# Two gated spectral filters on one core: a third fold for the even columns, row sums spread by broadcast stationary operands, the l = 512 products on GpSimd, and the inverse two pairs later

## The chip, the core and the metric

The kernel runs on one core of one Trainium2 chip. The core has five engines, each with an instruction queue of its own: TensorE (PE in the profile; PEld is its weight load), VectorE (DVE), ScalarE (ACT), GpSimd (POOL) and SyncE (SP), which here only starts transfers. They work on SBUF, 128 partitions wide; TensorE writes to PSUM, eight banks of 512 f32 columns, from which VectorE and ScalarE copy. Sixteen DMA engines move data. The metric is device time per execution in microseconds: the median of 3 runs before the change is 128.11 (127.71 to 128.34).

## The reference

One input x (2048 x 1024, bf16) goes through two filters, A and B, and a gate per row mixes them:

```python
X = rfft2(x)                      # over rows and columns, in f32
y = irfft2(X * (w_r + 1j * w_i))  # for A and for B, 2048 x 513 weights each
g = sigmoid((x * gate_w).sum(-1)) # one number per row
out = g * a + (1 - g) * b
```

Both filters share the forward transform, so there is one forward and one inverse chain; the gate enters the inverse as a factor on its coefficients.

## The kernel before

Work is written down operation by operation in program order; each names its engine, and waits are derived from which operations wrote or read the same piece. Each engine takes its operations strictly in that order, so the order of the calls sets what queues behind what. Nothing is planned by a scheduler.

**Load and stage 1.** x comes in eight pieces on SP's queue, then the weights in six groups (`wload`: columns t = 0; 1 to 3; 4 to 7; 8 to 11; 12, 13; 14, 15), 8.4 MB that are on their way until 48.7 us. VectorE folds each row twice (`fold`, L334): the row and its mirror image, as sum and difference. `stage1` multiplies with M (L369) and leaves the result in FT, in four blocks (`cmb`, for even and odd columns of the cosine and sine part) of two halves j. ScalarE copies most of PSUM to FT (L378), VectorE the rest (L376).

**Forward pairs.** 16 pairs i = (half hf, p), two t each. `step(i)` does `stage4(i)` (L442, eviction L446 to XF, the tile X), `swap(i)`, two DMAs that exchange the partitions of real and imaginary part (into MM, the tile XS; on GpSimd's queue for i < 8, on SP's from then on), and `stage2(i + 2)` (L418, eviction L427). Stage 2 sums over 256 folded columns for every l, in two matmuls j = 0, 1 of 128 columns each. X and XS have six slots. `product(i, sw)` on VectorE (L459) multiplies X (sw = 0) or XS (sw = 1) with the weights of both filters. Products of hf = 1 use column 512 of the weight rows, which the star products need first: so `star_products` (L493) waits for all weights, saves what it needs, and copies column 256 over column 512 (L496).

**Gate.** `gate_spectrum` (L471) sums the gate's products beside steps 0 to 5; `row_sums` makes 2048 row sums from these on VectorE (AT); `row_spread(hf)` (L502) lays half of them out on a diagonal mask, `zsum` (L508) sums this over partitions with a matrix of ones, ScalarE takes the sigmoid (L511), `gate_mask` (L517) splits it, and `rbgen(r)` (L548) multiplies it into the coefficients of row block r, from U5 (2 MB, loaded after the last stage 2 into FT).

**Inverse.** `group(u, g)` is 16 matmuls of 128 columns (L561) and one eviction (L571, on VectorE L569): 16 groups for hf = 0, which need all products of hf = 0, then 16 for hf = 1. `col0` (L535) corrects column 0 with the star products (PST); it stands before group 0, the last of hf = 0. From `STEP5 = 12` on, groups and steps alternate on TensorE. Then `stage6(r)` (L682, eviction L692) and `stage7(r)` (L707) for 16 row blocks. A row block of the usual kind makes four parts, which VectorE (L754) and then GpSimd (L759) add and subtract; one in `HALF` has VectorE do all of that, at more TensorE time; 14 and 15 are done on VectorE too. SP stores each block.

## Time and profile before

| | |
|---|---|
| median of 3 runs | 128.11 us |
| the profiled execution | 127.73 us, span 125.6 us |
| granted TensorE clock | 1.00 |
| TensorE / VectorE / ScalarE / GpSimd busy | 114.5 / 100.7 / 96.8 / 37.9 us |
| loads on the chain: x, weights | until 9.8 us, until 48.7 us |
| products on VectorE, 32 | 1.23 us each, L459 |
| first inverse group of hf = 1 | 73.03 us |
| first stage 6 | 89.88 us |
| GpSimd's 20 operations of stage 7 | 1.28 us each, 94.9 to 120.8 us |

Times inside the execution count from the span's start. The profiled execution is one of the program, with its span on the core and a little around it that the span does not hold (2.1 us). The chain of waits is followed back from the last instruction; a line of it names what the end was waiting for. A line number L... is that of the kernel before, shown above.

### The profile page before, as it was taken

To read this page: it belongs to the slowest core of one execution; us is meant where nothing else is said; L and a number is where in the kernel's file an instruction comes from. 1 tells how busy PE (TensorE), PEld (TensorE's weight loads), DVE (VectorE), ACT (ScalarE), POOL (GpSimd) and SP (SyncE) were. 2 spreads that over 40 slices of the span, in tenths; PEclk is the share of its full clock that TensorE was granted. 3 is DMA by queue.
4 is the path that set the end of the run, shared out by engine and by line. 5 is a ranking of instruction groups with operands and counts; after the bars stand their busy time and mean duration, and the time that the engine had idled before them with its cause. 6 is when DMAs were issued, how large, how long until landed. Compare 5 with 4: busy or idle time off the path is not lost.

```text
span 125.6 us, 3569 instructions
## 1 busy us (share of the span) xinstructions
PE 114.5 (91%) x1510; PEld 97.6 (78%) x1510; DVE 100.7 (80%) x145; ACT 96.8 (77%) x116; POOL 37.9 (30%) x45
## 2 busy tenths in 40 slices
PE   0399999999999999989999989999799999999980
PEld 0268787887767866979889989999799988998640
DVE  0578999355398988999999999999845788868892
ACT  4229985668989999989899998788669878686630
POOL 1000062006463900000000000000007999979940
PEclk9999999999999999999999999999999999999999
DMA  3999999999999998412894900000000224442366
GB/s 86 327 382 430 416 345 359 347 350 348 360 364 358 358 371 329 160 50 94 297 398 137 317 20 0 5 0 0 5 0 5 84 99 167 157 167 84 113 238 239
DMA packets 17503, 26.27 MB, mean 209 GB/s; under 512 B 2000, under 2 KB 10960, under 8 KB 17360
## 3 DMA queue, kind: packets, MB, share of 16 engines
q1 hardware_dynamic: 16512, 23.81, 54.2%
q0 software_dynamic: 832, 2.11, 4.7%
q8 instruction: 12, 0.20, 0.6%
q10 hardware_dynamic: 144, 0.13, 0.5%
q14 instruction: 3, 0.02, 0.1%
HBM read 17.64 MB, written 4.19 MB: 174 GB/s over the span
## 4 chain that ended last, share of the span: by engine, by line
PE 43%; DVE 28%; DMA 11%; SPq 10%; issue 3%; ACT 2%; DVEq 0%
PE PS L707 13%; PE PS L561 13%; PE PS L682 12%; SPq L280 10%; DVE WB L459 9%; DVE WA L459 8%; DMA WB<-in_A_x_dram 5%; DMA WA<-in_B_w_i_dram 5%; DVE XF L334 5%; DVE FT L376 2%; PE PS L369 2%; PE PS L442 1%; PE PS L418 1%; DVE WA L718 1%; DVE VD L502 1%
## 5 line engine op out<-in xcount | busy, mean ns | idle before, releaser
L759 POOL TENSOR_TENSOR WA<-WA 128x512 bf16<-128x512 f32 x20 | 24.9, 1276 | 51.8 <-DVE WA L754 51.7
L561 PE MATMUL PS<-CL,WB 128*128 128x128 bf16 x256 | 32.4, 226 | 0.5 <-ACT WB L571 0.5
L561 PEld LDWEIGHTS PS<-CL,WB 128*128 128x128 bf16 x256 | 31.5, 145 | 1.4 <-ACT WB L571 0.8
L561 PE MATMUL PS<-CL,WA 128*128 128x128 bf16 x256 | 32.3, 223 | 0.3 <-DVE WA L459 0.3
L561 PEld LDWEIGHTS PS<-CL,WA 128*128 128x128 bf16 x256 | 31.4, 145 | 0.8 <-DVE WA L459 0.5
L571 ACT ACTIVATE WB<-PS 128x1024 bf16<-128x1024 f32 (+1 forms) x29 | 27.8, 1012 | 3.3 <-PE PS L561 3.2
L459 DVE TENSOR_TENSOR WB<-XF,WA 128x2048 bf16<-128x2048 bf16 x16 | 19.6, 1230 | 3.7 <-ACT XF L446 3.4
L369 PE MATMUL PS<-MM,XF 128*128 128x256 bf16 x128 | 16.8, 297 | 5.6 <-DVE XF L334 5.2
L459 DVE TENSOR_TENSOR WA<-MM,WA 128x2048 bf16<-128x2048 bf16 x16 | 19.6, 1234 | 2.6 <-DMA MM<-XF 2.6
L692 ACT ACTIVATE WA<-PS 128x1024 bf16<-128x1024 f32 (+1 forms) x16 | 15.9, 998 | 6.7 <-PE PS L682 6.7
L369 PEld LDWEIGHTS PS<-MM,XF 128*128 128x128 bf16 x128 | 13.3, 106 | 8.9 <-DVE XF L334 5.2
L707 PE MATMUL PS<-FT,WA 128*128 128x256 bf16 (+1 forms) x132 | 19.7, 295 | 0.0
L446 ACT ACTIVATE XF<-PS 128x1024 bf16<-128x1024 f32 x16 | 16.7, 1044 | 2.5 <-PE PS L442 2.5
L754 DVE TENSOR_TENSOR WA<-PS,WA 128x512 f32<-128x512 f32 x20 | 12.9, 687 | 6.3 <-ACT WA L714 4.2
L418 PEld LDWEIGHTS PS<-F,FT 128*128 128x128 bf16 x256 | 15.1, 98 | 3.4 <-ACT XF L427 1.7
L418 PE MATMUL PS<-F,FT 128*128 128x128 bf16 x256 | 17.1, 219 | 0.0
L442 PE MATMUL PS<-XF,CK 128*128 128x512 bf16 (+1 forms) x72 | 16.4, 355 | 0.0
L427 ACT ACTIVATE XF<-PS 128x1024 bf16<-128x1024 f32 x15 | 15.8, 1051 | 0.3 <-PE PS L418 0.3
L707 PEld LDWEIGHTS PS<-FT,WA 128*128 128x128 bf16 x132 | 12.3, 98 | 3.6
L378 ACT ACTIVATE FT<-PS 128x1024 bf16<-128x1024 f32 x11 | 10.6, 1038 | 4.1 <-PE PS L369 4.1
L280 POOL DMA_DIRECT2D MM<-XF x16 | 8.8, 551 | 14.8 <-PE PS L442 8.6
L334 DVE TENSOR_TENSOR XF<-WB 128x512 bf16<-128x512 bf16 (+1 forms) x20 | 6.0, 367 | 6.0 <-DMA WB<-in_A_x_dram 6.0
(61 smaller groups left out, 118.4 us busy)
## 6 DMA issues: line engine op xcount, KB each, us to landing
out_dram<-WA SPq DMA_DIRECT2D x15, 256.0 KB, 2.1
MM<-XF POOLq DMA_DIRECT2D x16, 128.0 KB, 5.4
MM<-XF SPq DMA_DIRECT2D x16, 128.0 KB, 2.3
FT<-c_U SPq DMA_DIRECT2D x1, 2048.0 KB, 8.5
WB<-in_A_x_dram SPq DMA_DIRECT2D x3, 512.0 KB, 5.9
WA<-in_A_w_r_dram SPq DMA_DIRECT2D x4, 256.5 KB, 6.7
WA<-in_A_w_i_dram SPq DMA_DIRECT2D x4, 256.5 KB, 6.8
WA<-in_B_w_r_dram SPq DMA_DIRECT2D x4, 256.5 KB, 6.6
```

Source lines behind the costliest of these rows:

```text
L280: return P.add(eng, lambda e: e.dma_start(dst, src), dma=name, **kw)
L369: P.add("pe", lambda e, o=o, lh=lh, rh=rh, s=s: e.matmul(o, lh, rh, start=(s == 0), stop=(s == 1)), r=[("xf", c % 2, q, h, s), ("M", c), ( ...
L418: op = P.add("pe", lambda e, o=o, cmb=cmb, j=j, t=t, rh=rh: e.matmul(o, fblock(cmb, j, t), rh, start=(j == 0), stop=(j == 1)), r=[("F1", c ...
L427: P.add("act", lambda e: e.activation(dst, src, ACT.Copy), **kw)
L442: P.add("pe", lambda e, o=o, kind=kind, pm=pm, m=m, rh=rh: e.matmul(o, sl(CK, fbo(kind, pm, m), [(1, 128)]), rh, start=(m == 0), stop=(m = ...
L446: P.add("act", lambda e: e.activation(dst, ps(b0 * 512, [(256, 2), (512, 2), (1, 256)]), ACT.Copy), r=[bank(b0), bank(b0 + 1)], w=[("X", i ...
L459: P.add("dve", lambda e: e.tensor_tensor(out=at(sw), in0=sl(xt, xo, [(0, 2), (128, 8), (1, 128)]), in1=at(1), op=ALU.mult), r=[xk] + ["c25 ...
L561: P.add("pe", lambda e, o=o, l0=l0, ab=ab: e.matmul(o, sl(WT[ab], l0, [(RWS[ab] // 2, 128)]), sl(CL, KIo[ab], [(1, 128)]), start=(ab == 0) ...
L571: P.add("act", lambda e, s=src, d=dst: e.activation(d, s, ACT.Copy), r=b, a=["Z"])
L692: P.add("act", lambda e, s=src, d=dst: e.activation(d, s, ACT.Copy), **kw)
L707: P.add("pe", lambda e: e.matmul(ps(col, [(1, n * 256)]), lh, rh, start=(k == 0), stop=(k == last)), r=[("Y", r), "DI"] + ["DJ"] * (full o ...
L759: P.add("pool", lambda e, s=s, op=op: e.tensor_tensor(out=ods(s, 0, 2), in0=pv[:, :, 0, :], in1=pv[:, :, 1, :], op=op), r=[("PQ", pk, 0), ...
```

## The change

**Third fold.** For even columns, the folded row is folded once more: `fold3` on VectorE forms sum and difference of the two halves j, so each l needs one half only. Stage 2 then sums even columns over 128 instead of 256 and computes 64 columns per matmul instead of 128, with as many matmuls as before. The order of columns in `fold` and the matrix F2 change to suit, F2 is a quarter smaller, and the results lie in two new places (EO, and VD until the gate needs it) and for the rest in FT over what was folded. The gate's weights leave VD for the end of CL, so the load of CL's second part now waits for them. Two PSUM copies go from VectorE to ScalarE (last of stage 1, stage 2 of pair 1).

**Row sums.** `row_spread` and the matrix of ones go. `zsum` takes column n of the row sums (rounded to bf16, AB), repeated 128 times, as the stationary operand, and the mask as the moving one: 32 matmuls of 32 columns.

**l = 512.** `save512(k)` on GpSimd saves column 512 for one half of t and copies column 256 over it, for t < 8 behind swap 5 (weight groups 0 to 2) and for t >= 8 behind the swaps (weight groups 3 to 5). Products of hf = 1 wait for that half only. `star_products` goes to GpSimd, and the star column from step 6 to behind the first inverse group.

**Order.** Products follow a new list, `STEP5` is 14, and the groups of the inverse begin after stage 4 of pair 14. The first part of CL (CV) is loaded three weight groups earlier, and `HALF` has three row blocks instead of four. Constants GW and RG, not shown, follow the third fold.

```diff
-    dd = np.arange(256)[:, None]
-    F2 = np.zeros((4, 256, 256))
+    dd = np.r_[0:128, 255:127:-1][:, None]
+    F2 = []
...
-        F2[cmb] = np.cos(th) if cmb < 2 else np.sin(th)
-    C["F2"] = F2.reshape(4, 2, 128, 256).transpose(2, 0, 1, 3).reshape(128, 2048)
+        F = (np.cos(th) if cmb < 2 else np.sin(th)).reshape(2, 128, 256)
+        if par:
+            F2 += [F[0], F[1]]
+        else:
+            F = F[0].reshape(128, 2, 2, 32, 2)
+            e = [np.stack([F[:, :, 0, :, w], F[:, :, 1, :, 1 - w]], axis=2).reshape(128, 128) for w in range(2)]
+            F2 += e if cmb == 0 else e[::-1]
+    C["F2"] = np.concatenate(F2, axis=1)
...
+    EO = sb("EO", 1024)
+    W5 = sb("W5", 64)
...
+    AB = sb("AB", 32)
...
-    GR = VD
+    GRo = 1024
...
-    load("F2", F2, 0, 2048, cst["F2"].ap(), w=["F2"])
-    dma("sp", "GR", sl(GR, 0, [(1, 128)], np_=8), AP(gate_w.tensor, gate_w.offset, [[128, 8], [1, 128]]), r=["GRz"], a=["GR"])
+    load("F2", F2, 0, 1536, cst["F2"].ap(), w=["F2"])
+    dma("sp", "GR", sl(CL, GRo, [(1, 128)], np_=8), AP(gate_w.tensor, gate_w.offset, [[128, 8], [1, 128]]), r=["GRz"], a=["GR"])
...
-    P.add("pool", lambda e: e.tensor_copy(sl(GR, 128, [(1, 128)]), sl(GR, 127, [(-1, 128)])), r=["GR"], w=["GRr"])
+    P.add("pool", lambda e: e.tensor_copy(sl(CL, GRo + 128, [(1, 128)]), sl(CL, GRo + 127, [(-1, 128)])), r=["GR"], w=["GRr"])
...
-            i0 = sl(t, o + 511 * s, [(1024, n), (1 - 2 * s, 256)])
-            i1 = sl(t, o + (512 if s else 1023), [(1024, n), (2 * s - 1, 256)])
+            g = 1 - 2 * s
+            i0 = sl(t, o + 511 * s, [(1024, n), (256 * g, 2), (g, 128)])
+            i1 = sl(t, o + (512 if s else 1023), [(1024, n), (-256 * g, 2), (-g, 128)])
...
-                out=sl(XF, fo + h * 512 + s * 256, [(1024, n), (1, 256)]), in0=i0, in1=i1, op=ALU.subtract if h else ALU.add),
+                out=sl(XF, fo + h * 512 + s * 256, [(1024, n), (384 - 512 * s, 2), (1, 128)]), in0=i0, in1=i1, op=ALU.subtract if h else ALU.add),
...
     def folds(c):
...
-                                  r=[("xf", c % 2, q, h, s), ("M", c), ("NM", c)], w=[bank(2 * u + q // 2)])
+                                  r=[("xf", c % 2, q, h, s ^ j), ("M", c), ("NM", c)], w=[bank(2 * u + q // 2)])
...
                     src = ps(u * 1024, [(128, 2), (1, 128), (256, 4)])
...
-                    if (h == 1 and j == 0) or (c == 3 and h == 0 and j == 1):
+                    if (h == 1 and j == 0 and c < 3) or (c == 3 and h == 0 and j == 1):
...
     for k, (t0, t1) in enumerate(((0, 0), (1, 3), (4, 7), (8, 11), (12, 13), (14, 15))):
-        if t0 == 14:
+        if t0 == 8:
             load("CV", CL, 0, 576, cst["CL"].ap()[:, :576], w=["CV"])
         wload(k, t0, t1)
-    load("CL", CL, 576, CL.shape[1] - 576, cst["CL"].ap()[:, 576:], w=["CL"])
...
     def fblock(cmb, j, t):
-        return sl(FT, cmb * 4096 + j * 2048 + t * 128, [(1, 128)])
-    def stage2(i, css=(0, 1)):
+        if cmb in (1, 2):
+            return sl(FT, cmb * 4096 + j * 2048 + t * 128, [(1, 128)])
+        if t < 4:
+            return sl((EO, VD)[t // 2], cmb // 3 * 512 + j * 256 + t % 2 * 128, [(1, 128)])
+        return sl(FT, cmb * 4096 + j * 2048 + (t - 4) * 128, [(1, 128)])
+    def ekeys(i, cs, s):
+        return [("E", i, cs, s)] + ["VD"] * (i == 1)
+    def fold3(i, css=(0, 1)):
+        n = len(css)
+        for s, op in enumerate((ALU.add, ALU.subtract)):
+            src = [sl(FT, 12288 * css[0] + j * 2048 + i * 256, [(12288, n), (1, 256)]) for j in range(2)]
+            dst = sl(FT, 12288 * css[0] + s * 2048 + (i - 2) * 256, [(12288, n), (1, 256)]) if i > 1 else sl((EO, VD)[i], 512 * css[0] + 256 * s, [(512, n), (1, 256)])
+            P.add("dve", lambda e, dst=dst, src=src, op=op: e.tensor_tensor(out=dst, in0=src[0], in1=src[1], op=op),
+                  r=[("F1", cs, j) for cs in css for j in range(2)] + [("FR", i)], w=[("E", i, cs, s) for cs in css] + [("FR", i - 2)], a=["VD"] * (i == 1))
+    def stage2(i, css=(0, 1), ab=(0, 1)):
...
-        b0 = 4 if i == 1 else 6 if i in (9, 11, 13) else 0
-        for t in (2 * p, 2 * p + 1):
+        b0 = 4 if i == 1 else 6 if i in (9, 11, 13, 15) else 0
+        if 0 in ab:
             for cs in css:
-                for par in range(2):
-                    cmb = (0, 1, 3, 2)[2 * cs + par]
+                for t in (2 * p, 2 * p + 1):
...
-                        o = ps((b0 + t % 2) * 512 + cs * 256 + par * 64, [(64 if par else 192, 2), (1, 64)])
-                        rh = sl(F2, (cmb * 2 + j) * 256 + hf * 128, [(1, 128)])
-                        op = P.add("pe", lambda e, o=o, cmb=cmb, j=j, t=t, rh=rh: e.matmul(o, fblock(cmb, j, t), rh, start=(j == 0), stop=(j == 1)),
-                                   r=[("F1", cs, j), "F2"], w=[bank(b0 + t % 2)])
-        if css == (0,):
-            return op
+                        o = ps((b0 + t % 2) * 512 + cs * 256 + 64, [(64, 2), (1, 64)])
+                        rh = sl(F2, 256 + 512 * cs + 256 * j + hf * 128, [(1, 128)])
+                        P.add("pe", lambda e, o=o, cs=cs, j=j, t=t, rh=rh: e.matmul(o, fblock(1 + cs, j, t), rh, start=(j == 0), stop=(j == 1)),
+                              r=[("F1", cs, j), "F2"], w=[bank(b0 + t % 2)])
+        if 1 in ab:
+            for cs in css:
+                for t in (2 * p, 2 * p + 1):
+                    for w in range(2):
+                        v = 1 - w if cs else w
+                        o = ps((b0 + t % 2) * 512 + cs * 256 + v, [(193 - 2 * v, 2), (2, 32)])
+                        rh = sl(F2, 1280 * cs + w * 128 + hf * 64, [(1, 64)])
+                        op = P.add("pe", lambda e, o=o, cs=cs, t=t, w=w, rh=rh: e.matmul(o, fblock(3 * cs, w, t), rh, start=True, stop=True),
+                                   r=ekeys(p, cs, w) + ["F2"], w=[bank(b0 + t % 2)])
...
+        if css == (0,) or ab == (0,):
+            return
...
-        if i == 1:
-            P.add("dve", lambda e: e.tensor_copy(dst, src), **kw)
-        else:
-            P.add("act", lambda e: e.activation(dst, src, ACT.Copy), **kw)
+        P.add("act", lambda e: e.activation(dst, src, ACT.Copy), **kw)
         return op
...
-              r=[xk] + ["c256"] * hf + [("W", need[t]) for t in (2 * p, 2 * p + 1)], a=[("prod", sw, hf)])
+              r=[xk] + [("c256", p // 4)] * hf + [("W", need[t]) for t in (2 * p, 2 * p + 1)], a=[("prod", sw, hf)])
...
     def gate_spectrum(t):
         for m in range(8):
...
-                                                start=(m == 0), stop=(m == 7)), r=[("F1", m // 4, m % 2), "GW2"], w=[bank(6)])
+                                                start=(m == 0), stop=(m == 7)), r=["GW2"] + ([("F1", m // 4, m % 2)] if m // 2 in (1, 2) else ekeys(t // 2, m // 4, m % 2)), w=[bank(6)])
     def star_column(b):
...
+        P.add("dve", lambda e: e.tensor_copy(AB[:], AT[:]), r=["AT"], w=["AB"])
+    def save512(k):
+        at = lambda l: sl(WA, 16 * k * RW + l, [(32 * RW, 2), (RW, 16)])
+        wk = WK[3 * k:3 * k + 3]
+        P.add("pool", lambda e: e.tensor_copy(sl(W5, 16 * k, [(32, 2), (1, 16)]), at(512)), r=wk, w=[("W5", k)])
+        P.add("pool", lambda e: e.tensor_copy(at(512), at(256)), r=wk + [("W5", k)], w=[("c256", k)])
     def star_products():
         for sw in range(2):
-            P.add("dve", lambda e, sw=sw: e.tensor_tensor(out=sl(PST, sw * 64, [(32, 2), (1, 32)]), in0=sl(XST, 32 * sw, [(0, 2), (1, 32)]),
-                                                          in1=sl(WA, 512, [(32 * RW, 2), (RW, 32)]), op=ALU.mult),
-                  r=["XST", "XSS"] + WK, a=["PST"])
-        P.add("dve", lambda e: e.tensor_copy(sl(WA, 512, [(RW, 64)]), sl(WA, 256, [(RW, 64)])), r=["PST"], w=["c256"])
+            P.add("pool", lambda e, sw=sw: e.tensor_tensor(out=sl(PST, sw * 64, [(32, 2), (1, 32)]), in0=sl(XST, 32 * sw, [(0, 2), (1, 32)]),
+                                                           in1=sl(W5, 0, [(32, 2), (1, 32)]), op=ALU.mult),
+                  r=["XST", "XSS", ("W5", 0), ("W5", 1)], a=["PST"])
...
-    def row_spread(hf):
-        P.add("dve", lambda e: e.tensor_tensor(out=sl(VD, 0, [(1, 1024)]), in0=sl(CL, MKo + 32 * hf, [(1, 32), (0, 32)]),
-                                                in1=sl(AT, 0, [(0, 32), (1, 32)]), op=ALU.mult),
-              r=["AT", "CV"], w=["VD"])
     def zsum(u, hf):
-        for q in range(2):
-            P.add("pe", lambda e, q=q: e.matmul(ps(u * 1024 + q * 512, [(1, 512)]), sl(CL, ONo, [(1, 128)]),
-                                                sl(VD, q * 512, [(1, 512)]), start=True, stop=True),
-                  r=["VD", "CL"], w=[bank(2 * u + q)])
-        P.add("act", lambda e: e.activation(sl(VD, 0, [(1, 1024)]), ps(u * 1024, [(1, 1024)]), ACT.Sigmoid, scale=SM[:, 0:1]),
+        for n in range(32):
+            P.add("pe", lambda e, n=n: e.matmul(ps(u * 1024 + 32 * n, [(1, 32)]), sl(AB, n, [(0, 128)]), sl(CL, MKo + 32 * hf, [(1, 32)]),
+                                                start=True, stop=True),
+                  r=["AB", "CV"], w=[bank(2 * u + n // 16)])
+        P.add("act", lambda e: e.activation(sl(VD, 0, [(1, 1024)]), ps(u * 1024, [(1, 32), (32, 32)]), ACT.Sigmoid, scale=SM[:, 0:1]),
...
-    STEP5 = 12
+    STEP5 = 14
     for cs in range(2):
         for i in range(2):
-            stage2(i, (cs,))
-        if cs == 0:
-            gate_weights(7)
+            fold3(i, (cs,))
+        for ab in range(2):
+            for i in range(2):
+                stage2(i, (cs,), (ab,))
+            if cs == ab == 0:
+                gate_weights(7)
+    for i in range(2, 8):
+        fold3(i)
+    load("CL", CL, 576, CL.shape[1] - 576, cst["CL"].ap()[:, 576:], w=["CL", "GR", "GRr"])
...
         swap(i)
-        if i == 6:
-            star_column(7)
+        if i == 5:
+            save512(0)
         if i + 2 < 16:
             last2 = stage2(i + 2)
+        if i == 8:
+            save512(1)
         if i == 13:
             dma("sp", "U5", sl(FT, U5o, [(2048, 8), (1, 1024)]).bitcast(u16), cst["U5"].ap().rearrange("p (a b) -> p a b", a=8), w=["U5"], after=[last2])
+    ORDER = (((0, 0),), ((1, 0),), ((2, 0),), ((3, 0), (0, 1)), ((1, 1),), ((2, 1), (4, 0)), ((3, 1), (5, 0)), ((4, 1),),
+             ((5, 1),), ((6, 0), (6, 1)), ((8, 0),), ((7, 0), (7, 1), (8, 1)), ((9, 0), (9, 1)), ((10, 0), (10, 1), (11, 0), (11, 1)))
+    def products(i):
+        for n, sw in ORDER[i]:
+            product(n, sw)
...
-        for n, sw in (((0, 0),), ((1, 0),), ((2, 0),), ((0, 1), (3, 0)), ((1, 1), (2, 1), (4, 0)), ((3, 1), (5, 0)), ((4, 1), (6, 0)),
-                      ((5, 1), (6, 1), (7, 0), (7, 1)))[i]:
-            product(n, sw)
+        products(i)
...
-    star_products()
-    for i in range(8, STEP5):
-        product(i, 0)
-        product(i, 1)
-    row_sums()
-    row_spread(0)
-    slots = [2, 3]
+        products(i)
+        if i == 12:
+            row_sums()
+    slots = [2, 3, 0]
     def spare():
...
-    for i in range(STEP5, 16):
-        step(i)
-        if i < 14:
-            groups(3)
-        if i == 14:
-            slots.insert(0, 0)
-            groups(1)
-            u = spare()
-            for sw in range(2):
-                col0(u, sw)
-            groups(2)
-        if i == 15:
-            slots.insert(2, 1)
-            groups(1)
-            zsum(spare(), 0)
-        product(i, 0)
-        if i > 12:
-            product(i - 1, 1)
-    product(15, 1)
+    step(14)
+    groups(1)
+    star_column(2 * spare())
+    star_products()
+    groups(1)
+    for i in (12, 14):
+        for sw in range(2):
+            product(i, sw)
+    step(15)
+    slots.insert(3, 1)
+    groups(8)
+    for i in (13, 15):
+        for sw in range(2):
+            product(i, sw)
+    zsum(spare(), 0)
+    groups(2)
+    u = spare()
+    for sw in range(2):
+        col0(u, sw)
     gate_mask(0)
-    row_spread(1)
...
     groups(len(todo))
...
-    HALF = (4, 7, 11, 13)
+    HALF = (5, 8, 12)
...
     def stage7(r):
...
```

More of the change, by code (lines that the diff above doesn't have):

```diff
@@ L101, in make_consts @@
     blocks += [m[perm][:, perm] for m in (T1, T3, -T3, T3z, -T3z, T2, T4, -T4, T4z, -T4z)]
-    C["CL"] = np.concatenate([VR, MK.reshape(128, 64)] + blocks + [np.ones((128, 128))], axis=1)
+    C["CL"] = np.concatenate([VR, MK.reshape(128, 64)] + blocks, axis=1)
     l2, sl_, f = row % 2, (row // 2) % 32, row // 64
@@ L136, in make_consts @@
         for j in range(2):
-            RG[j, 0, cmb, j] += 1
-            RG[4 + j, 0, cmb, j] += sa * sb_
-            RG[7 - j, 1, cmb, j] += sa
-            RG[3 - j, 1, cmb, j] += sb_
+            RG[j, j, cmb, j] += 1
+            RG[4 + j, j, cmb, j] += sa * sb_
+            RG[7 - j, 1 - j, cmb, j] += sa
+            RG[3 - j, 1 - j, cmb, j] += sb_
+        if cmb in (0, 3):
+            RG[:, :, cmb] = 0.5 * np.stack([RG[:, :, cmb].sum(-1), RG[:, :, cmb, 0] - RG[:, :, cmb, 1]], axis=-1)
     GW = np.zeros((128, 4, 2, 2))
-    GW[:, 3, :, 1] = ((-1.0) ** np.arange(128))[:, None]
+    GW[:, 3, 1, 1] = (-1.0) ** np.arange(128)
     C["CK"] = np.concatenate(fb + [RG.reshape(128, 16), GW.reshape(128, 16)], axis=1)
@@ L270, in bass_gated_mix__spectral_gfnet__spectral_gfnet__prompt_kernel @@
     TO = [832 + 128 * j for j in range(10)]
-    ONo = 2112
     P = Prog()
@@ L291, in bass_gated_mix__spectral_gfnet__spectral_gfnet__prompt_kernel @@
     P.add("pool", lambda e: e.memset(DUM[:], 0.0), w=["DUM"])
-    P.add("pool", lambda e: e.memset(sl(GR, 0, [(1, 256)]), 0.0), w=["GRz"])
+    P.add("pool", lambda e: e.memset(sl(CL, GRo, [(1, 256)]), 0.0), w=["GRz"])
     def mload(eng, c0, n):
@@ L459, in product @@
         P.add("dve", lambda e: e.tensor_tensor(out=at(sw), in0=sl(xt, xo, [(0, 2), (128, 8), (1, 128)]), in1=at(1), op=ALU.mult),
-              r=[xk] + ["c256"] * hf + [("W", need[t]) for t in (2 * p, 2 * p + 1)], a=[("prod", sw, hf)])
+              r=[xk] + [("c256", p // 4)] * hf + [("W", need[t]) for t in (2 * p, 2 * p + 1)], a=[("prod", sw, hf)])
     def gate_weights(b):
         for n in range(2):
-            P.add("pe", lambda e, n=n: e.matmul(ps(b * 512, [(1, 8)]), sl(GR, 128 * n, [(1, 128)]), sl(CK, RGo + 8 * n, [(1, 8)]),
+            P.add("pe", lambda e, n=n: e.matmul(ps(b * 512, [(1, 8)]), sl(CL, GRo + 128 * n, [(1, 128)]), sl(CK, RGo + 8 * n, [(1, 8)]),
                                                 start=(n == 0), stop=(n == 1)), r=["GR", "GRr", "CK"], w=[bank(b)])
```

## The prediction

> **What bounds the kernel now.** I read first the busy shares, then the chain that ended last in order of time, then the timelines of VectorE and GpSimd, and last the waits.
>
> ```profile
> PE 114.5 (91%) x1510; PEld 97.6 (78%) x1510; DVE 100.7 (80%) x145; ACT 96.8 (77%) x116; POOL 37.9 (30%) x45
> ```
>
> No share settles it; each stretch has its own limit. The chain of waits:
>
> ```profile
> 26.47 0.89 PE PS L418 x16
> 27.36 0.38 PE PS L471 x16
> 27.74 0.90 PE PS L442 x4
> ...
> 42.16 6.53 DMA WA<-in_B_w_i_dram
> ...
> 51.16 0.39 DVE PST L493 x2
> ...
> 70.69 2.30 DVE WA L459 x2
> 72.99 0.05 issue
> 73.03 3.07 PE PS L561 x47
> 76.10 0.43 PE PS L508 x2
> 76.53 12.66 PE PS L561 x208
> ```
>
> Columns: start, length, work. To 48.7 the weights are on their way; from there to 73.0 VectorE works without a gap, 16 of its products held until the last weights and the star products (L493) are through; at 73.03 TensorE begins the second half of the inverse, 256 matmuls of L561, and stays the bound up to 121. So the change is worth what it does to the 73.03, plus what it does after it. A product is 1.145 us from start to start.
>
> What VectorE and GpSimd do to each other shows at one place only, here from their two timelines:
>
> ```profile
> 16.86 2.61 POOL L308 COPY VD<-VD 128x128 bf16<-128x128 bf16 x1 [15.78 <-DMA VD<-in_gate_w_dram]
> 16.56 2.76 DVE L334 TENSOR_TENSOR XF<-WA 128x512 bf16<-128x512 bf16 x8
> 19.24 3.59 DVE L376 CAST FT<-PS 128x1024 bf16<-128x1024 f32 x3
> ```
>
> GpSimd copies 128 columns and takes 2.61 us, though it fills 256 columns in 0.31 (L292) and does 512 columns of a two-input f32 operation in 1.28 (L759). The copy ends at 19.47, 0.15 after the eight folds end at 19.32; the folds, 0.335 apart, are not slowed. I read it so: a GpSimd operation that reads SBUF stands still while VectorE runs SBUF-to-SBUF operations back to back. GpSimd's DMA issues do not: at 40.9 to 44.1 they take 0.54 each beside products. Before, GpSimd has no other such operation until 94.9. The change gives it six in the middle of the products.
>
> **The change part by part.**
>
> *Even columns.* Per pair, 8 of the 16 matmuls of stage 2 fall from 128 to 64 columns. 16 of 128 take 0.89 (55.6 ns each), 16 of two columns 0.38 (23.7 each); 64 columns lie between 23.7 and 55.6, and I take 28, half of 55.6, which is above the floor. Saved: 0.22 per pair. In steps 0 to 5 TensorE sets the pace (2.188 per step, 27.60 to 38.54), so it becomes 1.97; afterwards ScalarE does (1.81 per step, its L427 from 40.70 to 51.57) and nothing is saved. Stage 4 of pair 14 ends at 52.8 by this, and the inverse begins there.
>
> *The third fold* adds 8 VectorE operations of 128x256 (286 ns, L334) and 12 of 128x512 (421); the second of each pair waits for the first, about 0.79 for a large pair: 23.5 to 29.4. VectorE idles there for 4.4 us (1.96, 1.55, 0.92 before its next three operations). Product (0,0) goes from 27.56 to 29.4, but the fifth product waits for a swap that lands at 34.4 either way, so the cost is 0, at most 1.8 were nothing caught up. Two PSUM copies that leave VectorE fall in ScalarE's idle 1.88 and 1.14.
>
> *Loads.* The CV load goes ahead of three weight groups on SP's queue: 0.65 for groups 3 and 4, landing at 37.6 and 43.5, wanted at 39.5 and 45.6: 0. The CL load waits for GpSimd's early copy and two matmuls, done by 24; it issues at 42.8 as before and is due at 50, ahead of the first group. The last weights still land at 48.7.
>
> *GpSimd's copies of columns 512 and 256* stand between the swaps of pairs 5 and 6 on its queue (and again behind pair 7). Swap 6, swap 7 are queued behind them; products (6,1), (7,1) wait for these. A swap is there 6.9 us after its X (27.5 to 34.54). With 1.97 per step X5 is ready at 37.35, GpSimd gets to its first copy at 38.8. VectorE began (2,1) at 38.35 and has five products to do, until 44.1; swap 5 lands at 44.25. That gap lets in the first copy at most; the second waits for the first, by then (5,1) and (6,0) run, to 46.7. Each copy costs 0.1 (the shortest row of GpSimd) to 0.31: the second ends at 47.0. Swap 6 issues to 48.1 and lands 2.0 (a swap of SP with quiet queues) to 5.4 us later (GpSimd's, beside the weights); I take 4.4, for the weights end at 48.7: 52.5. From there 19 products, 21.75, with the row sums, 1.36, and their copy, 0.34: VectorE ends its products at 75.95 in place of 72.95. What leaves it (0.8 of star products and copy, 1.2 of spreading) is in this count. ScalarE holds back X of pairs 12 and 13, whose slots swap 6, swap 7 and product (7,0) free, to 56.9, still ahead of the first group. The second pair of copies runs while VectorE waits for swap 6.
>
> *Star products on GpSimd.* The star column comes at 58.2 now, its copy at 59.8, two issues take 1.08 and the landing 5.1, as it did at 42.0: 66. Then two 64-column operations want SBUF while VectorE is in its last nine products. After these come gate mask, 1.04, and two rows of coefficients, 1.21, before VectorE stands at a copy that needs TensorE: 78.2. Two operations, 0.1 to 0.4 each, say 0.5: 78.7. TensorE is held at col0 by then (first group at 57.1 with product (7,1); twelve groups, pair 15 and the 32 small matmuls take it to 70.7). Then col0, 0.78, and four groups, 3.95: second half at 83.4, which is 10.4 later than 73.03.
>
> *Row sums spread by the stationary side:* 2 matmuls of 512 (0.43) become 32 of 32 columns, 24 to 28 ns each, 0.8: plus 0.4 for the one behind 73. VectorE's spread behind 73 (1.1) goes, but TensorE bounds that stretch: 0.
>
> *One half row fewer:* TensorE minus 0.43, GpSimd two more operations:
>
> ```profile
> 97.64 12.44 POOL L759 TENSOR_TENSOR WA<-WA 128x512 bf16<-128x512 f32 x10 [0.21 <-DVE WA L754]
> 110.82 9.99 POOL L759 TENSOR_TENSOR WA<-WA 128x512 bf16<-128x512 f32 x8 [0.75 <-DVE WA L754]
> ```
>
> At 2.49 per row, ten rows from 97.64 end at 122.5, not 120.8; row 13's store then opens the queue of the last four stores, 0.33 each, the last 0.2 later than now. Range minus 0.4 to plus 0.5; I take plus 0.2.
>
> Sum: 10.4 + 0.4 + 0.2 = 11.0. The profiled execution took 127.73 with its span of 125.6; that gives 138.7. It lies 0.4 under the median of 128.11, inside the ranges below.
>
> TensorE would idle some 8 us at col0. The granted clock is 1.00 in all stretches of this trace, the first matmuls after 5.2 us without work included. [...] By the row nothing is added.
>
> **The rivals.**
>
> *GpSimd slips in (faster).* If the shared resource is handed over between two VectorE instructions, each GpSimd operation waits at most one product. Two waits delay swap 6 by under 1 us and the star products by under 3, with col0 reached only at 66. Then VectorE ends at 70.2 to 71 and TensorE, from 52.8 with 16 groups (15.8), pair 15 (0.88), small matmuls (0.8), col0 and star (1.0), reaches the second half at 71.2: minus 1.8, plus 0.6: 126.5. For it: the copy is a single sighting. Against: seven handovers between folds went by unused. It stays faster as long as these waits hold TensorE up by less than 1.2 us. [...]
>
> *Only one of the two stalls.* If a late swap or other gap lets the copies through early, VectorE ends at 70.2 and the star products alone cost: 70.2 + 2.25 + 0.5 + 4.73 = 77.7, 133.0. If a gap behind 66 (pair 14's swap stands behind the 2 MB coefficient load, which takes 8.5) lets the star products through, 76.0 remains: 131.3.
>
> *The half-width matmuls are not faster* and GpSimd is not held: 1.3 later than the first rival, 127.8, no change.
>
> **How the numbers follow.** Both stalls 0.42 (135 to 140.5), one stall 0.24 (129.5 to 134.5), GpSimd slips in 0.27 (125.5 to 127.4), no change 0.06. Likeliest 138.7, its own range 135 to 140.5: the bounds of the swap's landing (minus 2.4, plus 1.0), and the clock above. Eight in ten needs the upper half of the faster case too: 126.3 to 140.5. Half a per cent is about what a measurement here can tell from no change: faster 0.27, same 0.06, slower 0.67.
>
> **What would show it.** Right: GpSimd's 32-column copies of over 1 us, the second ending just after a product; VectorE idle for 4 to 6 us ahead of (6,1) on a swap; TensorE waiting at col0 for GpSimd, whose star products end after the first rows of coefficients; second half of the inverse near 83. Stage 2 at 0.67 per pair, the 32 matmuls at 0.8. Wrong: GpSimd's operations short and beside products, second half near 71.

## The result and the profile after

The changed kernel takes 128.57 us (median), the kernel before 127.92: a ratio of 1.0051, interval 1.0028 to 1.0075, half a per cent slower. The profiled execution took 128.50 with a span of 126.7 (before 127.73 with 125.6). So the direction was right and the size was not: 11.0 us were forecast, 0.65 came. Two of the 13 executions, and two of the ten of e2 below, took 134.8 to 135.4 at a granted clock of 0.97; the ratios leave them out.

The busy shares moved little:

```profile
PE 113.5 (90%) x1570; PEld 97.9 (77%) x1570; DVE 101.6 (80%) x157; ACT 98.8 (78%) x118; POOL 43.0 (34%) x53
```

The chain that ended last, in order of time, shows where the time went. Columns: start, length, work. L443 are the odd and L452 the even columns of stage 2, L502 the gate's spectrum, L473 stage 4, L594 the inverse, L541 the spread row sums, L568 column 0, L725 stage 6:

```profile
26.35 0.95 PE PS L473 x8
27.30 0.45 PE PS L443 x8
27.74 0.45 PE PS L452 x8
28.19 0.38 PE PS L502 x16
28.57 0.89 PE PS L473 x4
...
65.34 0.79 PE PS L541 x32
66.13 1.99 PE PS L594 x32
68.12 0.76 PE PS L568 x16
68.88 6.85 PE PS L594 x112
75.73 0.79 PE PS L541 x32
76.52 12.71 PE PS L594 x208
...
89.91 1.96 PE PS L725 x32
```

Three things are to be seen. Stage 4 of pair 0, the first line, begins 0.8 later than before (25.53). The even columns take as long as the odd ones, 0.45 for eight, though a matmul has 64 columns instead of 128: a step, from one stage 4 to the next, is still 2.18 to 2.22 long (before 2.19). And TensorE works from 26.35 on without a pause until the second half: column 0 follows at 68.12 with nothing in front of it. Four groups (64 matmuls) are left of the first half at 68.88, 3.92 us, so the second half begins at 72.8, before at 73.03; stage 6 begins at 89.91, before at 89.88. All that was changed up to there comes to nothing in sum.

GpSimd between 40 and 66 us, from its timeline (start, length, line; in brackets what it waited for):

```profile
40.65 1.02 POOL L527 COPY W<-WA 128x32 bf16<-128x32 bf16 x1
41.73 1.23 POOL L528 COPY WA<-WA 128x32 bf16<-128x32 bf16 x1
42.81 2.17 POOL L290 DMA_DIRECT2D MM<-XF  x4
48.00 0.63 POOL L527 COPY W<-WA 128x32 bf16<-128x32 bf16 x1 [3.02 <-DMA WA<-in_B_w_i_dram]
48.69 0.33 POOL L528 COPY WA<-WA 128x32 bf16<-128x32 bf16 x1
...
63.68 1.88 POOL L532 TENSOR_TENSOR PST<-XST,W 128x64 bf16<-128x64 bf16 x2 [5.17 <-DMA XST<-XST]
```

The copies and star products do wait for VectorE, but each for one product at most (1.145 from start to start), not to the end of them; the two at 48, where VectorE waits for a swap, take 0.63 and 0.33. Swap 6 is issued behind two of them, at 42.81; product (6,1), which needs it, waits 0.26 for it. Neither this nor the star products hold TensorE.

What is left is the tail. First GpSimd's last operations, then SP's stores, after:

```profile
97.67 24.94 POOL L802 TENSOR_TENSOR WA<-WA 128x512 bf16<-128x512 f32 x20 [0.21 <-DVE WA L797]
```

```profile
122.63 0.33 SPq L290 DMA_DIRECT2D out_dram<-WA  x1
123.01 0.43 SPq L290 DMA_DIRECT2D out_dram<-WA  x1
123.49 0.45 SPq L290 DMA_DIRECT2D out_dram<-WA  x1
123.98 0.49 SPq L290 DMA_DIRECT2D out_dram<-WA  x1
```

VectorE's last six results of stage 7, after:

```profile
119.95 2.76 DVE L761 TENSOR_TENSOR WA<-PS,WA 128x512 bf16<-128x512 f32 x6
```

SP's queue and the same six results before:

```profile
121.22 0.43 SPq L280 DMA_DIRECT2D out_dram<-WA  x1
121.93 0.33 SPq L280 DMA_DIRECT2D out_dram<-WA  x1
122.59 0.39 SPq L280 DMA_DIRECT2D out_dram<-WA  x1
123.25 0.34 SPq L280 DMA_DIRECT2D out_dram<-WA  x1
```

```profile
120.62 2.60 DVE L718 TENSOR_TENSOR WA<-PS,WA 128x512 bf16<-128x512 f32 x6
```

GpSimd ends at 122.61 instead of 120.81. Before, the last three stores were 0.66 apart, each on VectorE's last results. Now VectorE is done 0.5 earlier (122.71, before 123.22), but four stores queue up behind GpSimd and go out one behind the other; the last is issued 0.73 later and its issue takes 0.15 longer.

### The profile page after: what moved, and what is told of

The parts are those of the page before. It is cut to its first block, busy times and chain, and to the rows that moved or that the text cites. A ratio compares the mean times of both kernels' runs of the same rounds, so it can differ in the third digit from the quotient of the medians.

```text
span 126.7 us, 3710 instructions
## 1 busy us (share of the span) xinstructions
PE 113.5 (90%) x1570; PEld 97.9 (77%) x1570; DVE 101.6 (80%) x157; ACT 98.8 (78%) x118; POOL 43.0 (34%) x53
## 4 chain that ended last, share of the span: by engine, by line
PE 77%; DVE 8%; DMA 5%; issue 2%; ACT 2%; SPq 2%; DVEq 0%
PE PS L594 25%; PE PS L750 13%; PE PS L725 11%; PE PS L473 11%; PE PS L452 6%; PE PS L443 5%; DMA WB<-in_A_x_dram 5%; DVE XF L345 5%; PE PS L502 2%; DVE FT L387 2%; SPq L290 2%; PE PS L380 2%; PE PS L541 1%; DVE WA L761 1%; ACT FT L389 1%
## 5 line engine op out<-in xcount | busy, mean ns | idle before, releaser
L802 POOL TENSOR_TENSOR WA<-WA 128x512 bf16<-128x512 f32 x22 | 27.3, 1291 | 29.7 <-DVE WA L797 29.6
L594 PE MATMUL PS<-CL,WB 128*128 128x128 bf16 x256 | 31.9, 226 | 0.0
L594 PE MATMUL PS<-CL,WA 128*128 128x128 bf16 x256 | 31.7, 223 | 0.0
L594 PEld LDWEIGHTS PS<-CL,WB 128*128 128x128 bf16 x256 | 31.3, 145 | 0.5 <-issue 0.4
L594 PEld LDWEIGHTS PS<-CL,WA 128*128 128x128 bf16 x256 | 31.3, 145 | 0.1
L380 PE MATMUL PS<-MM,XF 128*128 128x256 bf16 x128 | 16.0, 288 | 6.6 <-DVE XF L345 5.4
L380 PEld LDWEIGHTS PS<-MM,XF 128*128 128x128 bf16 x128 | 12.8, 103 | 9.5 <-DVE XF L345 5.3
L797 DVE TENSOR_TENSOR WA<-PS,WA 128x512 f32<-128x512 f32 x22 | 14.2, 686 | 6.7 <-ACT WA L757 4.2
L477 ACT ACTIVATE XF<-PS 128x1024 bf16<-128x1024 f32 x16 | 17.2, 1078 | 1.6 <-PE PS L473 1.6
L458 ACT ACTIVATE XF<-PS 128x1024 bf16<-128x1024 f32 x16 | 16.8, 1058 | 0.9 <-PE PS L452 0.9
L473 PE MATMUL PS<-XF,CK 128*128 128x512 bf16 (+1 forms) x72 | 16.7, 358 | 0.0
L290 POOL DMA_DIRECT2D MM<-XF x16 | 8.8, 555 | 17.1 <-PE PS L473 12.1
L389 ACT ACTIVATE FT<-PS 128x1024 bf16<-128x1024 f32 x12 | 11.5, 1025 | 3.2 <-PE PS L380 3.2
L443 PEld LDWEIGHTS PS<-F,FT 128*128 128x128 bf16 x128 | 8.0, 98 | 3.8 <-ACT XF L458 2.1
L443 PE MATMUL PS<-F,FT 128*128 128x128 bf16 x128 | 10.0, 220 | 0.0
```

The lines of the kernel that those rows point to most:

```text
L380: P.add("pe", lambda e, o=o, lh=lh, rh=rh, s=s: e.matmul(o, lh, rh, start=(s == 0), stop=(s == 1)), r=[("xf", c % 2, q, h, s ^ j), ("M", c ...
L443: P.add("pe", lambda e, o=o, cs=cs, j=j, t=t, rh=rh: e.matmul(o, fblock(1 + cs, j, t), rh, start=(j == 0), stop=(j == 1)), r=[("F1", cs, j ...
L458: P.add("act", lambda e: e.activation(dst, src, ACT.Copy), **kw)
L473: P.add("pe", lambda e, o=o, kind=kind, pm=pm, m=m, rh=rh: e.matmul(o, sl(CK, fbo(kind, pm, m), [(1, 128)]), rh, start=(m == 0), stop=(m = ...
L477: P.add("act", lambda e: e.activation(dst, ps(b0 * 512, [(256, 2), (512, 2), (1, 256)]), ACT.Copy), r=[bank(b0), bank(b0 + 1)], w=[("X", i ...
L594: P.add("pe", lambda e, o=o, l0=l0, ab=ab: e.matmul(o, sl(WT[ab], l0, [(RWS[ab] // 2, 128)]), sl(CL, KIo[ab], [(1, 128)]), start=(ab == 0) ...
```

## The experiments

Four questions: what the tail costs, why the even columns were not faster, what GpSimd's copies cost, and, since one row of the profile had misled the forecast, what that row was. e1 to e4 ran together, beside 20 runs of before (median 127.91), e5 and e6 beside 6 (127.77). e5 and e7 to e12 are one execution each, run for the profile; with their added work they take 128.4 to 133.7, and nothing is read from that.

**e1_contiguous: even columns written without gaps.** The changed kernel writes the 64 even columns of a matmul to every second place of PSUM, so that ScalarE's copy puts them in order with the odd ones. Here every matmul of stage 2 writes runs of 32 columns, the odd ones too, and the copy puts them in order.

```diff
-            F2 += [F[0], F[1]]
+            F2 += [f.reshape(128, 4, 32, 2).transpose(0, 1, 3, 2).reshape(128, 256) for f in F]
...
-                        o = ps((b0 + t % 2) * 512 + cs * 256 + 64, [(64, 2), (1, 64)])
+                        o = ps((b0 + t % 2) * 512 + cs * 256 + 32, [(96, 2), (64, 2), (1, 32)])
...
-                        o = ps((b0 + t % 2) * 512 + cs * 256 + v, [(193 - 2 * v, 2), (2, 32)])
+                        o = ps((b0 + t % 2) * 512 + cs * 256 + 64 * v, [(224 - 128 * v, 2), (1, 32)])
...
-        dst, src = sl(XF, CSo(i), [(1, 1024)]), ps(b0 * 512, [(128, 8), (1, 64), (64, 2)])
+        dst, src = sl(XF, CSo(i), [(1, 1024)]), ps(b0 * 512, [(128, 8), (1, 32), (32, 4)])
```

> The changed kernel with the results of the even columns written to PSUM in contiguous runs of 32 instead of every second column (odd columns regrouped too, and the eviction reads the four runs in turn, so the values are the same). Theory W: the 64-column matmuls take 56 ns because they write every second PSUM column. Then the 8 of a pair take 0.20 to 0.25 us instead of 0.45, steps 0 to 5 fall from 2.19 to about 1.97, TensorE could begin the second half of the inverse at 71.3 and VectorE, whose products then end at 71.5 to 72, lets it begin there instead of at 72.8: span 125.5 to 126.0, time 127.3 to 127.8, ratio to the kernel before 0.995 to 0.999. Theory L: 56 ns is what any matmul of 64 or more columns with weights of its own takes. Then the 8 stay at 0.45, nothing moves, ratio 1.003 to 1.008.

Measured: 127.65, ratio 0.9983 (0.9962 to 1.0005), level with before and below the changed kernel, as theory W had it. From its chain:

```profile
27.01 1.02 ACT XF L477
28.03 0.93 ACT XF L458
28.96 0.05 issue
29.00 0.62 PE PS L443 x8
29.62 0.23 PE PS L452 x8
```

Eight matmuls of even columns now take 0.23, some 29 ns each; the forecast had 28. But ScalarE, which copies stage 4 (L477) and stage 2 (L458) out of PSUM, appears on the chain: the next matmuls wait for its copies. A step of the first six is 2.08, not 1.97, and later ones are 1.83, at about ScalarE's pace (two copies in 1.81), where the changed kernel's are 1.76. Of the 0.22 for each of 16 pairs, 3.5 us, 1.0 reaches stage 6, at 88.93.

**e2_old_half, e3_both, e4_before_new_half: the half rows.** e2 is the changed kernel with the four half rows of before, e3 that and e1 together, e4 the kernel before with the three of the changed one.

```diff
# e2_old_half and e3_both
-    HALF = (5, 8, 12)
+    HALF = (4, 7, 11, 13)
# e4_before_new_half
-    HALF = (4, 7, 11, 13)
+    HALF = (5, 8, 12)
```

> The changed kernel with HALF back at (4, 7, 11, 13). Theory P: the 1.1 us by which the span is longer all come from GpSimd's eleventh row, whose store opens the last four. Then GpSimd ends at 120.8 instead of 122.6, the last store is issued at 123.3 instead of 124.0, span 125.6 to 125.9, ratio to the kernel before 0.997 to 1.001. Rival: the end is set by TensorE and the stores, and one half row more costs TensorE its 0.43: ratio 1.005 to 1.009.

> Both edits together. If W and P hold, their gains add, for they lie on either side of the 16 inverse groups: span 124.4 to 125.0, time 126.3 to 126.9, ratio 0.987 to 0.992. If only P holds 0.997 to 1.001, if neither 1.003 to 1.009.

> The kernel before with nothing changed but HALF = (5, 8, 12). Theory P: GpSimd ends at 122.5, span 126.4 to 126.8, ratio 1.005 to 1.009. Rival (TensorE bounds the end): 0.43 less, ratio 0.996 to 0.998.

Measured: e2 127.88, ratio 0.9994 (0.9969 to 1.0018); e3 127.05, 0.9943 (0.9921 to 0.9965); e4 128.77, 1.0073 (1.0045 to 1.0102). GpSimd's last operations in e2, e3 and e4:

```profile
110.84 9.99 POOL L802 TENSOR_TENSOR WA<-WA 128x512 bf16<-128x512 f32 x8 [0.75 <-DVE WA L797]
```

```profile
109.94 10.00 POOL L802 TENSOR_TENSOR WA<-WA 128x512 bf16<-128x512 f32 x8 [0.76 <-DVE WA L797]
```

```profile
97.89 24.94 POOL L759 TENSOR_TENSOR WA<-WA 128x512 bf16<-128x512 f32 x20 [0.21 <-DVE WA L754]
```

With four half rows GpSimd has a gap to wait in (0.75) and ends at 120.83 and 119.94; with three it works through and ends at 122.83. This one line makes the kernel before 0.86 slower, and taken back it makes the changed kernel level with before: it accounts for the whole loss, as theory P had it. e3 beats both kernels, by 0.86 against before. It is less than was expected of it, 126.3 to 126.9. Against the changed kernel's 128.57 e1 gains 0.92, e2 0.69 and both 1.52: the two nearly add, and each alone is inside what was expected of it. Those ranges together allowed 1.3 to 2.3; that of e3 began at 1.7 and was too narrow.

**e6_step2: the price of the step, in the kernel before.** If gaps are what costs, they must cost in matmuls that have nothing to do with the third fold.

```diff
-                        o = ps((b0 + t % 2) * 512 + cs * 256 + par * 64, [(64 if par else 192, 2), (1, 64)])
+                        o = ps((b0 + t % 2) * 512 + cs * 256 + par, [(129 - 2 * par, 2), (2, 64)])
...
-        dst, src = sl(XF, CSo(i), [(1, 1024)]), ps(b0 * 512, [(128, 8), (1, 64), (64, 2)])
+        dst, src = sl(XF, CSo(i), [(1, 1024)]), ps(b0 * 512, [(1, 1024)])
```

> The kernel before, with one thing changed: stage 2 writes its 128 columns for each matmul to PSUM in steps of two (even to even places, odd to odd), and ScalarE reads them back in order; the same values, as many matmuls, as many columns. Theory W (a matmul that writes PSUM in steps of two takes twice the time for each column, whatever it computes): a stage-2 matmul goes from 56 to 100 to 112 ns, 16 of them from 0.89 to 1.6 to 1.8, a step of the first six from 2.19 to 2.9 to 3.1, and the time up by 4 to 13 us. Theory N (the 64-column matmuls of the changed kernel were slow for another reason, such as their alternation or their small size): 16 still take 0.89, the step stays at 2.19, time within 0.5%.

Measured: 139.76, ratio 1.0946 (1.0885 to 1.1006), as theory W had it. From its chain:

```profile
29.96 0.89 PE PS L442 x4
30.84 1.77 PE PS L418 x16
32.62 0.38 PE PS L471 x16
33.00 0.89 PE PS L442 x4
```

16 matmuls of 128 columns take 1.77 instead of 0.89, 110.6 ns each instead of 55.6, a step 3.04. The same values in the same number of columns cost twice the time when they go to every second place, here as with 64 columns (56 against 29 ns). A jump between runs shows no such price: the 55.6 are of columns in two runs of 64 with a jump between them, the 29 in two runs of 32, which makes 0.43 and 0.45 ns a column, and the four matmuls of stage 4 above, of 512 columns in one run each, take 0.43 a column too (L442, 0.89 for the four).

**e5_copies: GpSimd beside folds and beside products.** The kernel before with copies that nobody reads, and with the gate's own copy moved behind the folds (not shown):

```diff
-        for (q0, n), h in todo:
+        for k, ((q0, n), h) in enumerate(todo):
             fold(c, q0, n, h)
+            if c == 3 and k == 0:
+                P.add("pool", lambda e: e.tensor_copy(sl(PRB, 0, [(1, 32)]), sl(MM, 0, [(1, 32)])), r=[("M", 0)], after=[last_fold[3]])
+                P.add("pool", lambda e: e.tensor_copy(sl(PRB, 32, [(1, 128)]), sl(MM, 0, [(1, 128)])), r=[("M", 0)])
...
-        product(i, 0)
+        op = product(i, 0)
+        if i == 8:
+            for o, n, st in ((160, 32, 1), (192, 32, 1), (224, 128, 1), (352, 128, -1), (480, 512, 1)):
+                P.add("pool", lambda e, o=o, n=n, st=st: e.tensor_copy(sl(PRB, o, [(1, n)]), sl(F2, 0 if st > 0 else n - 1, [(st, n)])), r=["F2"], after=[op])
```

> The kernel before, with added copies on GpSimd that nothing reads: while VectorE does the folds of piece 3 (0.335 us each, back to back), one of 32 and one of 128 columns behind the first of these folds, and the gate's copy of 128 reversed columns behind them; and behind the first of VectorE's second set of products (1.145 us each) copies of 32, 32, 128, 128 (reversed) and 512 columns. The kernel's outputs are unchanged. Question: why the gate's copy stood 2.61 and 2.95 us beside the folds when the copies of 32 columns beside products took 0.25 to 1.25. Theory H (a copy gets its turn when VectorE goes from one instruction to the next): every copy takes at most one VectorE instruction and its own 0.2 to 0.6, so under 0.7 in the folds (32 and 128 columns alike) and 0.2 to 1.8 beside the products. Theory C (each hand-over lets only some columns through; 128 columns in eight folds make 16 for each): in the folds 32 columns take some 0.7 and 128 some 2.6; beside products 32 take 2.3, 128 take 9, and 512 don't end before the products do. Theory S (short instructions back to back don't hand over, long ones do): in the folds even the 32 columns stand to the end of the run of folds, 1.5 to 2.6; beside products all are done in 0.2 to 1.8.

From the timelines of GpSimd and VectorE at 17 us, and last the row of the five copies beside products (ns, least, median and most):

```profile
17.52 2.02 POOL L349 COPY PRB<-MM 128x32 bf16<-128x32 bf16 x1 [16.44 <-DVE XF L334]
19.48 0.29 POOL L350 COPY PRB<-MM 128x128 bf16<-128x128 bf16 x1
```

```profile
16.71 2.76 DVE L334 TENSOR_TENSOR XF<-WA 128x512 bf16<-128x512 bf16 x8
19.39 3.58 DVE L381 CAST FT<-PS 128x1024 bf16<-128x1024 f32 x3
```

```profile
L620 POOL COPY PRB<-F x5: 1142/1295/1610, 53.4 to 58.1; 128x32 bf16<-128x32 bf16 x2, 128x128 bf16<-128x128 bf16 x2, 128x512 bf16<-128x512 bf16 x1
```

At 17 us even 32 columns stand until the folds are over (19.47), past six of them; beside VectorE's copies from PSUM 128 columns then take 0.29. Beside products 32, 128 and 512 columns each take one product: 1.14 to 1.61. That falls in with theory S, and against H and C.

**e7_split, e8_split_back, e9_forward: is it the length, or the reading backwards?** e7 is e5 with products of pairs 8 to 11 in four operations each; e8 lets these read X backwards, and so pairs other columns; e9 is e5 with the folds of piece 3 reading forward, which pair other columns too.

```diff
# e7_split, in product
+        if i in range(8, 12):
...
+            for k2 in range(2):
+                for h in range(2):
+                    pt = lambda k, k2=k2, h=h: sl(WT[k], (4 * p + 32 * k2 + 2 * h) * RWS[k] + 128 * hf, [(RWS[k] // 2, 4), (1, 128)])
+                    ops.append(P.add("dve", lambda e, pt=pt, h=h: e.tensor_tensor(out=pt(sw), in0=sl(xt, xo + 512 * h, [(128, 4), (1, 128)]), in1=pt(1), op=ALU.mult),
...
# e8_split_back, within the last line
-in0=sl(xt, xo + 512 * h, [(128, 4), (1, 128)])
+in0=sl(xt, xo + 512 * h + 127, [(128, 4), (-1, 128)])
# e9_forward, in fold
+            if c == 3:
+                i0 = sl(t, o + 256 * s, [(1024, n), (1, 256)])
+                i1 = sl(t, o + 768 - 256 * s, [(1024, n), (1, 256)])
```

> The kernel with the added GpSimd copies, with the eight products of pairs 8 to 11 each split into four VectorE operations of 512 columns (some 0.335 us apart, as the folds are, 32 of them); GpSimd's five copies stand behind the first of these. The same values, no other change; VectorE needs some 0.2 more for each split product. Question: whether it is the length of VectorE's operations that decides if GpSimd gets in between. Theory L (length): the first copy, of 32 columns, stands until VectorE's run of short operations ends, up to 10 us, and the others follow after it. Theory K (something else tells folds from products, their tiles or their directions): every copy waits at most one short operation, all five are done within 3 us. Theory Q (a hand-over only where VectorE's operation has a wait of its own, which the first of each four has and the folds don't): one copy for every product, 1.3 to 1.4 apart, done within 7.

> As the run with eight split products, but these operations read their X operand backwards, 128 columns at a time from the last to the first, as one operand of each fold is read. The eight products then have columns in the wrong order, so the result differs from the reference; work and traffic are the same. Theory R (it is the operand read backwards that keeps GpSimd out): the first copy, of 32 columns, stands until the run of short operations ends, up to 10 us. Theory O (something else about the folds): all five copies are done in 2.3 us, as with forward reading.

> The kernel with the added GpSimd copies (products whole), with the folds of piece 3 reading both operands forward instead of one of them backwards; the sums of piece 3 then pair the wrong columns, so the result differs from the reference; as many operations of as many columns. Theory R: the 32-column copy in these folds takes at most one fold and its own time, 0.3 to 0.7 in place of 2.02. Theory O: it stands to the end of the folds again, 1.8 to 2.2.

GpSimd's five copies in e7 with eight of VectorE's operations, the first four beside them, and the first copy in the folds of e9:

```profile
52.29 2.31 POOL L628 COPY PRB<-F 128x32 bf16<-128x32 bf16 x5 [7.75 <-DVE WB L470]
```

```profile
53.19 2.03 DVE L470 TENSOR_TENSOR WA<-MM,WA 128x512 bf16<-128x512 bf16 x4
55.14 1.43 DVE L470 TENSOR_TENSOR WB<-XF,WA 128x512 bf16<-128x512 bf16 x4
```

```profile
17.61 2.02 POOL L352 COPY PRB<-MM 128x32 bf16<-128x32 bf16 x1 [16.52 <-DVE XF L337]
```

In e7 all five get through within 2.31 us beside operations as short as the folds, in e8 as well (2.31), and the forward folds of e9 keep the copy out as before. So theory S falls, and so do L and Q of e7 and R of e8 and e9; neither the length nor the direction decides it.

**e10_late_folds, e11_idle_folds, e12_both_places: the place.** e10 puts eight operations of the folds' shape among the products, e11 right behind the folds of piece 3, each with GpSimd's copies behind the first (not shown). In both, the eight wrote one place and waited for each other, so they tell little; in e12 they write two places by turns, and it has eight at both.

```diff
+            for k in range(8):
+                s_ = k % 2
+                i0 = sl(F2, 511 * s_, [(1024, 2), (1 - 2 * s_, 256)])
+                i1 = sl(F2, 512 if s_ else 1023, [(1024, 2), (2 * s_ - 1, 256)])
+                f = P.add("dve", lambda e, k=k, i0=i0, i1=i1: e.tensor_tensor(
# e10_late_folds (behind the folds, in e11_idle_folds: PRB for VD and MM for F2)
+                    out=sl(VD, (k % 2) * 256, [(512, 2), (1, 256)]), in0=i0, in1=i1, op=ALU.subtract if k % 4 > 1 else ALU.add), r=["F2"], w=["VD"])
# e12_both_places, at both
+                    out=sl(PRB, (k % 2) * 256, [(512, 2), (1, 256)]), in0=i0, in1=i1, op=ALU.subtract if k % 4 > 1 else ALU.add), r=["F2"], w=[("PRB", k % 2)])
```

> The kernel with the added GpSimd copies (products whole), with eight more VectorE operations behind the first of the second set of products, made as the folds of piece 3 are (two operands of 2x256 columns, one read backwards, 0.335 apart, results that nobody reads), and GpSimd's five copies behind the first of these. VectorE needs some 2.8 more. Question: whether it is the fold as an instruction that keeps GpSimd out, or where it stands. Theory I (the instruction): the first copy, of 32 columns, stands 1.8 to 2.4, to the end of the eight. Theory P (the place: what else runs at 17 us): the first copies take 0.3 to 0.5 each, at least four of them done within the eight.

> The kernel before, with eight more VectorE operations straight behind the folds of piece 3, of the folds' shape, whose results nobody reads, so that TensorE is signalled by none of them; GpSimd's copies of 32 and 128 columns stand behind the first of these eight. The folds themselves have no copy beside them but the gate's. VectorE is some 2.8 later for what follows. Question: whether the place keeps GpSimd out or that each fold signals TensorE. Theory G (the signals): the 32 columns take 0.2 to 0.5 here. Theory T (the time and place, what the other engines and the transfers do at 17 to 22 us): they stand 1.8 to 2.6, to the end of the eight.

> In the last two kernels the eight added operations wrote one place and so each waited for the one ahead of it: 8 took 3.96 and 3.74 where the folds take 2.76, and that pause may be what let GpSimd in. Here they write two places by turns and wait only for the last but one. Eight of them stand straight behind the folds of piece 3, and eight behind the first of the second set of products; behind the first of each eight, GpSimd copies 32 and 128 columns (early) and 32 and 32 (late). The eight should take 2.8 at both places, if nothing gets in. Theory D (the pause let GpSimd in): without it the first copy stands to the end of the eight, 1.8 to 2.6, early and late. Theory T (time and place): 1.8 to 2.6 early, 0.3 to 0.5 late. Theory F (something in the real folds, such as their waits for TensorE): 0.3 to 0.5 at both places, and each copy adds some 0.1 to 0.3 to the eight.

The first copy took 0.46 in e10 and in e11, as theories P and G had it; but the eight took 3.96 and 3.74, with pauses. In e12, GpSimd and VectorE, early and then late:

```profile
20.11 2.35 POOL L357 COPY PRB<-MM 128x32 bf16<-128x32 bf16 x1 [19.03 <-DVE PRB L353]
```

```profile
19.63 2.76 DVE L353 TENSOR_TENSOR PRB<-MM 128x512 bf16<-128x512 bf16 x8
```

```profile
56.15 0.68 POOL L636 COPY PRB<-F 128x32 bf16<-128x32 bf16 x2 [8.93 <-DVE PRB L631]
```

```profile
55.66 2.79 DVE L631 TENSOR_TENSOR PRB<-F 128x512 bf16<-128x512 bf16 x8
```

The same eight operations, at the same pace, keep GpSimd out at 20 us and let two copies through at 56, as theory T (time and place) had it and theories D and F did not. Theory G falls too, for these eight signal TensorE of nothing, as those of e11. With e11, where pauses went with a short copy at 20 us, it fits that GpSimd gets no turn there unless VectorE pauses. But the place is not shown to be the cause. It is one profile of each kernel, the early copies read MM and the late ones F2, and transfers, ScalarE and TensorE do other work; none of these was tried alone. And the same place gives both results: in the profiles of the changed kernel and of e1, e2 and e4 the gate's copy took 0.29 to 0.39, beside the same kind of folds. e4 is the kernel before in all but stage 7, and its copy and folds are these, where the kernel before had 2.61:

```profile
16.90 0.39 POOL L308 COPY VD<-VD 128x128 bf16<-128x128 bf16 x1 [15.82 <-DMA VD<-in_gate_w_dram]
```

```profile
16.40 2.86 DVE L334 TENSOR_TENSOR XF<-WA 128x512 bf16<-128x512 bf16 x8
```

So the row that the forecast stood on did not come back in another execution of what is the same code up to there. What decides it stays open.

## Why the prediction was right or wrong

**What bounds the kernel: right for the kernel before, half right after.** The end follows the second half: it begins at 72.8 in the changed kernel and at 71.8 in e1, and stage 6 follows 17.1 later in both. But what sets its begin is no longer VectorE, whose last product ends at 72.37; it is TensorE's own first half, which is without a pause.

**Even columns: wrong.** The step that failed is "I take 28, half of 55.6". The measured 56 is its upper bound, 55.6; the choice did not look at where the result goes: in steps of two, as the diff shows. e1 and e6 show the price. The 0.22 saved per pair became nothing. And had they been 29, the step would not have been 1.97: the forecast counted TensorE alone, and e1 has 2.08 with ScalarE on the chain.

**Third fold, loads: right.** VectorE's third folds end at 29.9 (29.4 forecast) and its first product starts at 29.81; it still waits 1.89 for a swap at 40.35, so its delay is made good by then, though not at the fifth product, as forecast, which followed at 36.09 without a wait. The last weights are there at 48.0, and the CL load lands at 49.7 (50 forecast). A small cost was missed: stage 4 of pair 0 begins at 26.35 instead of 25.53, and TensorE has no pause behind it to make that good. No run tells how much of it is the third fold and how much the new order.

**GpSimd's copies and star products, 10.4 of the 11.0: wrong.** The step that failed is "a GpSimd operation that reads SBUF stands still while VectorE runs SBUF-to-SBUF operations back to back". It was one row, at 17 us, read as a rule and carried to 40 to 78 us. The profile of the changed kernel and e5 show what holds there: at most one product for each operation (1.02 and 1.23 for the copies at 40 us, 1.14 to 1.61 in e5, a product being 1.145 from start to start). So the second copy ended at 42.96, not 47.0, and column 0 was not held. The rival "GpSimd slips in", with 0.27, had this mechanism right. It does not hold everywhere: nine copies at 17 to 22 us, beside operations 0.335 apart, took 2.0 to 2.95 and stood through six to eight of these. The forecast had both readings before it and took the row's side for all of the kernel.

**Row sums: right.** 0.8 was forecast for the 32 matmuls, 0.79 came.

**One half row fewer: mechanism right, size off.** Plus 0.2 was taken; e4 measured 0.86, e2 some 0.7. GpSimd's end was right (122.5, measured 122.61). Mis-sized was the queue of the last four stores: "0.33 each" came out as 0.38, 0.48 and 0.49 from one to the next, and the last issue takes longer too, 0.49. Both measured costs lie above the term's range, minus 0.4 to plus 0.5.

**The rival that came true** had 0.06: half-width matmuls not faster and GpSimd not held, 127.8. With the tail at its measured size, 0.5 to 0.7 more than was taken, that is 128.3 to 128.5; the profiled execution took 128.50. The measured median lay inside the stated range, at a place the cases gave little to, and the direction was right by luck: slower was forecast for column 0 waiting on GpSimd, and came from the stores. (The likeliest case's own range also began lower, at 135, than the bound that it names: 138.7 less 2.4 is 136.3.) Its upper end, 140.5, counts a slower TensorE clock behind a wait at column 0, a term that no run shows. In its place the changed kernel showed no such wait: TensorE is busy without a gap from 26.35 to 72.8, at a granted clock of 1.00, and the clock of 0.50 in its profile comes at 124.2, 2.8 behind the last matmul, which ends at 121.44.

## What to carry to other kernels

Before a matmul is priced by its columns, look at how its result lies in PSUM: columns written in steps of two cost twice as much here (110.6 against 55.6 ns for 128), as much as halving them would save; let the copy out of PSUM put them in order instead. A stall seen in one row is evidence for that execution and that place; a change that would be stopped by it deserves the rival that it does not hold elsewhere a chance to match, and two or three copies put beside the real work show what holds there. And when two engines share the tail, a small shift of work between them is worth what the last store does, queue and all, which here was more than all else in the change came to.

## What the runs showed of the hardware that was not expected

- PSUM in steps of two: 56 ns for 64 columns against 29 in runs of 32, 110.6 for 128 against 55.6 in runs of 64.
- GpSimd's copies beside VectorE's products of 1.145 us: 0.25 to 1.25 for 32 columns, 1.61 for 512. Beside operations of 0.335 us: five copies in 2.31 at 52 us, but 2.0 to 2.95 for one at 17 to 22 us in nine of the profiles, and 0.29 to 0.39 in four others.
- GpSimd slows VectorE in turn: four short operations beside copies of e7 took 2.03 instead of 1.43, and a product of e5 beside the copy of 512 columns 1.64 instead of 1.23.
